# Sliding-window attention into a cosine-gated feed-forward: the opening rewritten as one list of steps, with the first two token tiles in halves

## The chip, the cores and the metric

The kernel runs on one core of a Trainium2 chip. A core has TensorE (PE, matrix multiplies into PSUM), VectorE (DVE), ScalarE (ACT, functions such as exponential and sine), GpSimd (POOL) and SyncE (SP), each with its own instruction stream in order, and 16 DMA engines that move data on request of a queue. GpSimd's queue can convert f32 to bf16 on the way; SyncE's queue copies and transposes. The metric is the device time of one execution in microseconds. The kernel before takes 308.19 us, the median of 3 runs (308.08 to 308.48).

## What is computed

Eight batches, eight heads of 64, 576 tokens each. Every token attends to itself and the 63 tokens before it; the heads of a token are then put side by side and go through two matrix products with a gate between them.

```python
scores = scale * np.matmul(q, k.transpose(0, 1, 3, 2))      # q, k, v: (8, 8, 576, 64) f32
mask = (rel >= 0) & (rel < 64)                               # rel = query position - key position
scores = np.where(mask, scores, -1000000000.0)
attn = softmax(scores)                                       # max subtracted, exp, divided by the sum
x = matmul(attn, v).transpose(0, 2, 1, 3).reshape(4608, 512)
h = x @ w_in                                                 # w_in (512, 2048)
out = (h * np.cos(h)) @ w_out                                # w_out (2048, 512)
```

## The kernel before

**Tiles.** The 4608 tokens are cut into nine tiles of 512 for the feed-forward. Attention works in units of 64 queries against 128 keys for two heads at once (a "pair", four pairs); a batch has nine units per pair, so that tile 1 covers the last 64 tokens of batch 0 and the first 448 of batch 1. Three or four units make a group, and a group passes through these steps, each a function: scores (`g_scores`, `burst`, PE), negated row maximum (`g_max`, DVE), exponential with row sums (`g_exp`, ACT), reciprocal (`g_inv`, DVE), normalisation to bf16 `w` (`g_norm`, GpSimd or DVE), transposition of `w` to `wT` (`g_trans`, on PE with a copy out of PSUM by `g_put`, or by SyncE's DMA). Then `values` multiplies by v into `o_ps` and `put_x` copies that to `xT`, the feed-forward's input.

**Feed-forward.** For each of 16 blocks of 128 columns of w_in, four matmuls of 512 tokens (`first`, L351) make h in a PSUM bank; ACT takes the sine of h + pi/2 (L507), DVE multiplies it with h (the gate, L510) into `gT`. Then 16 matmuls for each 128 tokens (L522) give the output, which is copied out of PSUM and stored. Five named PSUM banks (X0, X1, S, O0, O1) and three taken in turn ("t") are shared by all of this.

**Order.** Everything is scheduled by hand: what one engine does follows the order in which the program issues it. From tile 1 on, the steps of the next batch's attention are put into a plan with due times (`at`), and `pump` issues what is due after each sine block or four output matmuls. The opening, which has nothing to hide behind, is the string `FIRST` (L41): steps of batch 0's attention in order, such as `s.0.1` (scores of pair 0, second group), `m`, `e`, `i`, `n`, `w`, `c` (the steps above), `tq`/`tk` and `pq`/`pk` (transposition of q and k on PE, copy out of PSUM), `z` (v shifted by 64 tokens, by DVE or GpSimd), `v` and `x` (values, xT), `h` (three or more first-layer blocks over one pair), `l` (the next load), `tb` (table of the sine).

**Batch 0 before.** All q, k and v rows come by GpSimd's queue, cast on the way, pair by pair for batch 0; q is scaled when it is copied out of PSUM. The causal window is added on PE: a matmul of `ident` with `mask16` (L238) starts each group's PSUM bank, and `g_max` is a plain reduction (L273); the exponential reads the scores in PSUM. For batch 1 on, `g_max` (L277) adds the mask and takes the maximum at once, writing `s` to SBUF, from where the exponential reads. Loads of w_in come in three pieces after v, then q and k of batch 1, then w_out in two, all early in GpSimd's order.

**Tile 0 and 1 before.** Tile 0's first layer starts block by block over pairs (`skewed`), its output layer runs in two halves of the 16 blocks; batch 1's scores and softmax are in the plan at fixed times during tile 0.

Of the kernel before, what the change touches and what calls it, by code (L numbers as in the profile page):

```python
# [10 lines left out]
def _safe_warn(msg, *a, **kw):  # L11
# [22 lines left out]
T = 2 * Q  # L34
LAGS = (0.2, 1, 3, 3.2, 3.8)
SKEW = 3
DIRECT = (0, 1, 2, 3, 8, 9)
# [14 lines left out]
def kernel(  # L52
# [35 lines left out]
    mask16 = const.tile([128, 6, 128], BF16, name="mask16")  # L88
# [7 lines left out]
    H_FIRST = ("O1", "X0", "X1", "S", "O0") * 3 + ("X0",)  # L96
    H_SECOND = ("X0", "X1", "S", "O0", "O1") * 3 + ("t",)
    H_BANKS = ("X0", "O0", "X1", "S", "O1") * 2 + ("X0", "X1", "S", "O0", "O1", "t")
    S_BANKS = ("X1", "S", "X0")
    BURSTS = (("X0", "X1", "S", "t"), ("X0", "X1", "S", "t", "t", "t"))  # L100
    S_FIRST = ("O1", "S", "O0", "X0", "X1")
# [16 lines left out]
    def put_masks():  # L118
        nc.vector.tensor_tensor(out=mask[:, 2], in0=mask[:, 0], in1=mask[:, 0], op=ALU.mult)
        nc.vector.tensor_scalar(mask[:, 1], mask[:, 2], 64.0 ** 2, NEG, ALU.is_gt, ALU.mult)  # L120
        nc.vector.tensor_scalar(mask[:, 2], mask[:, 1], -1.0, NEG, ALU.mult, ALU.add)
        nc.vector.tensor_copy(mask[:, 0, 0:64], mask[:, 2, 0:64])
        nc.vector.memset(mask[:, 0, 64:128], NEG)
        for lo, hi, of in ((0, 3, 0), (3, 5, 1), (5, 6, 1)):
            nc.scalar.copy(mask16[:, lo:hi], mask[:, of:of + hi - lo])

# [53 lines left out]
    def transposed(name, b, ps_):  # L180
# [7 lines left out]
        for p, t in zip(ps_, t_ps):  # L188
            st["t" + name, b, p] = t

    def put(name, b, p, engine=None):
        of = st.pop(("t" + name, b, p)).rearrange("d (c p) -> d p c", c=RC)
        to = halves(turned(b))[name][:, p].rearrange("d (p c) -> d p c", c=RC)
        if b or name == "k":
            copy(engine, to, of)
        elif engine == "a":
            nc.scalar.mul(to, of, scale)
        else:
            nc.vector.tensor_scalar(to, of, scale, None, ALU.mult)
# [31 lines left out]
    direct = set(range(n_first)) | {n_first + i for i in DIRECT}  # L231

    def g_scores(n, which):
        s_ps = bank(S_FIRST[which], "s_ps")
        units = groups[n]
        s_ps = s_ps[:, 0:len(units) * 128].rearrange("p (u c) -> p u c", c=128)
        m0 = 2 if units[0][2] else 0
        nc.tensor.matmul(out=s_ps.rearrange("p u c -> p (u c)"), lhsT=ident,  # L238
                         rhs=mask16[:, m0:m0 + len(units)].rearrange("p u c -> p (u c)"),
                         start=True, stop=False, skip_group_check=True)  # L240
        for u, (b, p, j) in enumerate(units):
            for h in range(2):
                d = slice(64 * h, 64 * h + 64)
                nc.tensor.matmul(out=s_ps[d, u].rearrange("p (a t) -> p a t", a=2), lhsT=q_cols(b, p, j)[d],
                                 rhs=k_cols(b, p, j)[d], start=False, stop=u == len(units) - 1, skip_group_check=True)
        st["s", n] = s_ps
        st.update({("cross", unit): 0 for unit in units})


    def burst(n0, banks):  # L250
        for i in range(0, len(banks), 2):
            pair = [groups[n0 + i], groups[n0 + i + 1]]
# [3 lines left out]
            for u in range(len(pair[0])):  # L256
                for cross in range(2):
# [6 lines left out]
                    st["cross", (b, p, j)] = cross ^ (p % 2 if b == 1 else 0)  # L264
            for cross in range(2):
                st["s", n0 + i + cross] = s_ps[cross]


    def g_max(n):
        s_ps, units = st["s", n], groups[n]  # L270
        negm = att.tile([128, GF], F32, tag="negm", name="negm", bufs=8)
        if n < n_first:
            nc.vector.tensor_reduce(out=negm[:, 0:len(units)], in_=s_ps, op=ALU.max, axis=AX.X, negate=True)  # L273
        else:
            s = att.tile([128, GF, 128], F32, tag="s", name="s", bufs=4)
            for u, (b, p, j) in enumerate(units):
                nc.vector.tensor_tensor_reduce(out=s[:, u], in0=s_ps[:, u], in1=mask[:, 2 - j % 2 if j else 0],  # L277
                                               scale=-scale if b else -1.0, scalar=BIG, op0=ALU.add, op1=ALU.min,
                                               accum_out=negm[:, u:u + 1])
            st["s", n] = s  # L280
        st["m", n] = negm

    def g_exp(n):
        s, negm = st.pop(("s", n)), st.pop(("m", n))
        e = att.tile([128, GF, 128], F32, tag="e", name="e", bufs=6)
        den = att.tile([128, GF], F32, tag="den", name="den", bufs=8)
        for u in range(len(groups[n])):
            nc.scalar.activation(e[:, u], s[:, u], AF.Exp, bias=negm[:, u:u + 1], scale=1.0 if n < n_first else -1.0,  # L288
# [3 lines left out]
    def g_inv(n):  # L292
        e, den = st["e", n]
        rden = att.tile([128, GF], F32, tag="rden", name="rden", bufs=8)
# [40 lines left out]
    def put_x(mt, p, engine=None):  # L335
        if ("xT", mt) not in st:
            st["xT", mt] = att.tile([128, PAIRS, MT], BF16, tag="xT", name="xT", bufs=2)
        o_ps = st.pop(("o", mt, p))
        copy(engine, st["xT", mt][:, p], o_ps)
# [8 lines left out]
    def first(mt, ff, ks, start, stop):  # L348
        if start:
            st["h", ff] = bank((H_FIRST, H_SECOND, H_BANKS)[min(mt, 2)][ff], "h_ps")  # L350
# [3 lines left out]
    def skew(mt):  # L354
        return 5 if mt == 1 else SKEW

    def skewed(mt, ks, n):
        for ff in range(skew(mt)):
# [206 lines left out]
```

## Time and profile before

| | |
|---|---|
| median of 3 runs | 308.19 us (308.08 to 308.48) |
| the profiled execution | 308.04 us, span 306.0 us |
| PE busy | 294.1 us, 96% |
| ACT busy | 235.6 us, 77% |
| DVE busy | 219.3 us, 72% |
| GpSimd busy | 171.9 us, 56% |
| moved by DMA | 43.58 MB, mean 142 GB/s |

In a timeline row the first number is the start from the span's begin, the second how long the instruction or the merged run of instructions took, then engine, line, operation, output<-input, shapes, count, and in brackets the idle time before it and what released it. In a row of the chain the second number is the time that this piece holds the chain. In a row of DMA issues the last number is the time from issue to landing. Matmuls are pipelined, so their listed durations overlap; their spacing tells what one costs. A row of a stretch of time lists the busy time of PE, weight loads, DVE, ACT and GpSimd with their counts, the granted TensorE clock as a share of full speed, the DMA share and the GB/s.

### The profile page before, as it was taken

How to read it: one execution, taken by the hardware profiler on the slowest of the kernel's cores; microseconds unless marked ns; L12 is line 12 of the kernel's file. 1: busy time of each engine (PE TensorE's matmuls, PEld its weight loads, DVE VectorE, ACT ScalarE, POOL GpSimd, SP SyncE). 2: the span in 40 equal slices, each digit the busy share in tenths (PEclk: the TensorE clock that was granted, in tenths of full speed). 3: DMA queues.
4: the chain of work that ended last, by engine and by line, in shares of the span. 5: the costliest groups of instructions: out<-in, count | busy, mean ns of one | idle time of the engine just before them, and what ended most of it. 6: DMA issues, size and time to landing. Idle time of an engine off the chain costs nothing.

```text
span 306.0 us, 7884 instructions
## 1 busy us (share of the span) xinstructions
PE 294.1 (96%) x2668; PEld 143.1 (47%) x2668; DVE 219.3 (72%) x832; ACT 235.6 (77%) x786; POOL 171.9 (56%) x200
## 2 busy tenths in 40 slices
PE   3979999999999999999999999999999999999996
PEld 2645444444444444444454445444544454454443
DVE  2796889678787778777878787788778877235701
ACT  4798689977997799879986998699869987106600
POOL 8997237889465976497759765957533630000000
PEclk9989999999999999999999999999999999999999
DMA  6999999599969999999999999999993441011012
GB/s 83 167 211 207 208 168 161 79 179 166 238 110 159 180 197 135 164 149 219 145 170 161 213 141 170 161 216 120 171 170 117 88 130 61 0 72 70 0 69 71
DMA packets 165577, 43.58 MB, mean 142 GB/s; under 512 B 154720, under 2 KB 161056, under 8 KB 165536
## 3 DMA queue, kind: packets, MB, share of 16 engines
q0 software_dynamic: 99632, 18.36, 75.4%
q1 hardware_dynamic: 65760, 24.52, 39.9%
q8 instruction: 21, 0.34, 0.5%
q10 hardware_dynamic: 144, 0.20, 0.2%
q14 instruction: 20, 0.16, 0.2%
HBM read 36.70 MB, written 9.44 MB: 151 GB/s over the span
## 4 chain that ended last, share of the span: by engine, by line
PE 83%; ACT 5%; DVE 5%; DMA 3%; POOL 1%; issue 1%; POOLq 0%; DVEq 0%
PE h_ps L351 41%; PE out_ps L522 33%; ACT e L288 3%; PE o_ps L330 3%; PE s_ps L261 3%; DMA rows<-in_q_dram 1%; PE out_ps L366 1%; DVE s L277 1%; DMA wT<-w 1%; DVE negm L273 1%; DVE w L302 1%; ACT L343 1%; PE tk_ps L186 1%; PE tq_ps L186 1%; POOL w L302 1%
## 5 line engine op out<-in xcount | busy, mean ns | idle before, releaser
L351 PE MATMUL h_ps<-xT,w_in 128*128 128x512 bf16 x576 | 128.1, 381 | 0.9 <-ACT xT L109 0.5
L522 PE MATMUL out_ps<-w_out,gT 128*128 128x512 bf16 x560 | 125.1, 379 | 0.2 <-DVE gT L510 0.2
L510 DVE TENSOR_TENSOR gT<-h_ps,sin 128x512 bf16<-128x512 f32 x144 | 95.5, 689 | 35.4 <-ACT sin L507 35.2
L507 ACT ACTIVATE sin<-h_ps 128x512 f32<-128x512 f32 x144 | 83.0, 599 | 34.2 <-PE h_ps L351 33.0
L288 ACT ACTIVATE e<-s,negm 128x128 f32<-128x128 f32 x256 | 98.6, 387 | 0.3 <-DVE negm L277 0.3
L302 POOL TENSOR_TENSOR w<-e,rden 128x512 bf16<-128x512 f32 (+1 forms) x76 | 74.3, 992 | 32.4 <-DVE rden L295 30.3
L351 PEld LDWEIGHTS <-w_in 128*128 128x128 bf16 x576 | 55.9, 98 | 66.7 <-issue 2.0
L522 PEld LDWEIGHTS <-gT 128*128 128x128 bf16 x560 | 53.2, 98 | 62.4 <-issue 0.2
L277 DVE CUSTOM_DVE_ANT_0 s<-s_ps,mask 128x128 f32<-128x128 f32 x256 | 58.1, 285 | 0.4 <-PE s_ps L261 0.4
L288 ACT ACTIVATION_READ_ACCUMULATOR e<-s,negm 128x1 f32 x256 | 48.0, 188 | 0.0
L149 POOL DMA_DIRECT2D rows<-in_q_dram x30 | 25.4, 866 | 25.3 <-DMA T<-rows 15.5
L162 POOL DMA_DIRECT2D v<-in_v_dram x35 | 29.6, 869 | 12.4 <-DMA rows<-in_k_dram 5.8
L109 ACT COPY out_sb<-out_ps 128x512 f32<-128x512 f32 (+1 forms) x18 | 10.1, 561 | 24.4 <-PE out_ps L522 19.0
L295 DVE RECIPROCAL rden<-den 128x4 f32<-128x4 f32 (+1 forms) x80 | 13.8, 172 | 18.3 <-ACT e L288 17.1
L149 POOL DMA_DIRECT2D rows<-in_k_dram x30 | 25.5, 898 | 0.5 <-DMA T<-rows 0.5
L109 DVE CAST xT<-o_ps 128x512 bf16<-128x512 f32 x26 | 16.9, 681 | 6.5 <-PE o_ps L330 6.2
L277 DVE DVE_READ_ACCUMULATOR2_ANT negm<- 128x1 f32 x256 | 21.3, 83 | 0.0
L109 DVE COPY out_sb<-out_ps 128x512 f32<-128x512 f32 x18 | 12.4, 689 | 12.0 <-PE out_ps L522 12.0
L288 ACT ACTIVATE e<-s_ps,negm 128x128 f32<-128x128 f32 x32 | 11.4, 394 | 1.6 <-DVE negm L273 1.4
L261 PE MATMUL s_ps<-T 64*64 64x128 bf16 x512 | 12.1, 221 | 0.0
L261 PEld LDWEIGHTS <-T 64*64 64x64 bf16 x512 | 8.2, 106 | 8.3 <-DVE negm L277 3.9
L330 PEld LDWEIGHTS <-v 128*64 128x64 bf16 x504 | 9.7, 114 | 4.4 <-issue 2.3
(54 smaller groups left out, 148.9 us busy)
## 6 DMA issues: line engine op xcount, KB each, us to landing
out_dram<-out_sb SPq DMA_DIRECT2D x16, 512.0 KB, 6.9
v<-in_v_dram POOLq DMA_DIRECT2D x28, 128.0 KB, 8.3
rows<-in_q_dram POOLq DMA_DIRECT2D x24, 128.0 KB, 5.9
rows<-in_k_dram POOLq DMA_DIRECT2D x24, 128.0 KB, 9.0
w_out<-in_moe_w_out_dram POOLq DMA_DIRECT2D x2, 1024.0 KB, 16.8
w_in<-in_moe_w_in_dram POOLq DMA_DIRECT2D x2, 768.0 KB, 12.1
wT<-w SPq DMA_TRANSPOSE x66, 3.8
out_dram<-out_sb SPq DMA_DIRECT2D x3, 256.0 KB, 2.0
```

Of the source, the lines that this page charges most:

```text
L109: {"a": nc.scalar.copy, "p": nc.gpsimd.tensor_copy}.get(engine, nc.vector.tensor_copy)(out, in_)
L149: nc.gpsimd.dma_start(out=rows(b)[lo:lo + n, slot * 512:slot * 512 + 512].rearrange("p (h d) -> p h d", h=H), in_={"q": q, "k": k}[name][b ...
L162: nc.gpsimd.dma_start(out=vt.rearrange("p (h d) -> p h d", h=H), in_=v[b, :, c * 128:c * 128 + n, :].rearrange("h p d -> p h d"))
L261: nc.tensor.matmul(out=s_ps[cross][to, u].rearrange("p (a t) -> p a t", a=2), lhsT=q_cols(b, p, j)[d], rhs=k_cols(b, p, j)[d], start=True, ...
L277: nc.vector.tensor_tensor_reduce(out=s[:, u], in0=s_ps[:, u], in1=mask[:, 2 - j % 2 if j else 0], scale=-scale if b else -1.0, scalar=BIG, ...
L288: nc.scalar.activation(e[:, u], s[:, u], AF.Exp, bias=negm[:, u:u + 1], scale=1.0 if n < n_first else -1.0, accum_out=den[:, u:u + 1])
L302: (nc.gpsimd if engine == "p" else nc.vector).tensor_tensor(out=w[:, 0:u], in0=e[:, 0:u], op=ALU.mult, in1=rden[:, 0:u].unsqueeze(2).to_br ...
L330: nc.tensor.matmul(out=o_ps[64 * h:64 * h + 64, 64 * i:64 * i + 64], lhsT=values_of(b)[:, max(j - 1, 0), 128 * p + 64 * h:128 * p + 64 * h ...
L351: nc.tensor.matmul(out=st["h", ff], lhsT=w_in_sb[:, ks, ff * 128:ff * 128 + 128], rhs=st["xT", mt][:, ks], start=start, stop=stop)
L507: nc.scalar.activation(sin, h_ps, AF.Sin, bias=math.pi / 2.0)
L510: nc.vector.tensor_tensor(out=gt[:, e], in0=h_ps, in1=sin, op=ALU.mult)
L522: nc.tensor.matmul(out=o_ps[e], lhsT=gT[ff // 2][:, ff % 2, ms * 128:ms * 128 + 128], rhs=w_out_sb[:, ff], start=ff == 0, stop=ff == n_ff - 1)
```

## The change

The opening becomes one list that reaches through tile 0, batch 1's attention and the first blocks of tile 1; a function `step` reads each token of it, loads included.

- Tiles 0 and 1 go through values, xT, first layer, sine and gate in halves of 256 tokens, with two blocks of 128 columns in one bank (`half_values`, `half_x`, `half_first`, `half_sin`, `half_gate`). Tile 0 takes its second half first. A half block is 8 matmuls of 256 columns; sine and gate still handle 512 columns at once. Its token `hh` issues the two pairs that come first, `hi` the other two. Tile 0's output layer is issued by fours of blocks (`o.ms.part`), between batch 1's scores.
- k and q of pair 0 are loaded as f32 by SyncE (`k0h`, `q0h`) into an output tile and cast to bf16 by ACT (`ck0:a`, `cq0:a`).
- The mask matmul and `mask16` go; batch 0 uses the masked maximum and reads `s` in SBUF like the others, and q is not scaled on its way any more.
- v of batch 0 is shifted by SyncE's DMA in three parts (`z.1`, `z.0`, `z.2`).
- w_in and w_out are loaded in quarters (`wi0` to `wi3`, `wo0` to `wo3`). `wi0` and `wi1` follow v's chunks 2, 3, 1; `wi3`, then batch 1's k and q (`kB`, `qB`), then `wi2` stand between normalisations on GpSimd; then come chunks of batch 2's q and k, w_out and batch 1's v (`vB`).
- Six of batch 1's groups for tile 1 have `w` transposed by DMA (`BY_DMA`), four groups for tile 1 on PE; before it were six on PE.

```diff
-DIRECT = (0, 1, 2, 3, 8, 9)
+BY_DMA = (11, 12, 13, 15, 16, 17)
 FIRST = (
...
+    "k0h q0h k1 id q1 q3 iota ck0:a k3 cq0:a tk.0 q2 pk.0:d tq.0 k2 tk.1 pq.0:a v2 mask pk.1:a s.0.1:O1 v3 tq.1 "
+    "m.0.1 s.0.0:X0 pq.1:a v1 tq.3 m.0.0 e.0.1 s.1.1:X1 wi0 tk.3 m.1.1 s.1.0:S wi1 pq.3:a pk.3:d tq.2 e.1.1 i.0.1 "
+    "s.3.1:O0 pq.2:d n.0.1:p tk.2 m.3.1 pk.2:a v0 w.0.1 s.2.1:O1 i.1.1 e.3.1 c.0.1:d n.1.1:p s.2.0:X0 m.2.1 z.1 "
+    "w.1.1 i.3.1 e.2.1 m.2.0 n.3.1:p s.3.0:X1 c.1.1:d w.3.1 e.0.0 i.2.1 m.3.0 n.2.1:p v.0.1 wi3 c.3.1:a w.2.1 "
+    "x.0.1:d e.2.0 c.2.1:d hh.0.1:O0 i.0.0 hh.1.1:O1 m.1.0 n.0.0:p v.1.1 e.3.0 hh.2.1:X0 x.1.1:d kB w.0.0 i.2.0 "
+    "z.0 hh.3.1:X1 n.2.0:d e.1.0 qB hi.0.1 hi.1.1 c.0.0:d wi2 w.2.0 i.3.0 hi.3.1 i.1.0 tb n.3.0:p n.1.0:d hi.2.1 "
+    "hh.7.1:S c.2.0:d q2c4 w.1.0 sin.0.1 w.3.0 c.1.0:d k2c4 hi.7.1 sin.2.1 g.0.1 v.0.0 sin.1.1 c.3.0:d q2c3 "
+    "hh.6.1:O0 v.1.0 x.0.0:a g.1.1 wo0 hi.6.1 sin.7.1 g.2.1 hh.0.0:O1 v4 sin.6.1 Bk.0 x.1.0:d hh.1.0:X0 wo1 "
...
+    "x1.0.1:a w1.18 v1.1.1 sn1.4 x1.1.1:a g1.4 w1.19 sn1.3 g1.3 g1.2 "
 )
...
     def g_scores(n, which):
-        nc.tensor.matmul(out=s_ps.rearrange("p u c -> p (u c)"), lhsT=ident,
-                         rhs=mask16[:, m0:m0 + len(units)].rearrange("p u c -> p (u c)"),
-                         start=True, stop=False, skip_group_check=True)
...
     def g_max(n):
-        if n < n_first:
-            nc.vector.tensor_reduce(out=negm[:, 0:len(units)], in_=s_ps, op=ALU.max, axis=AX.X, negate=True)
...
+            nc.vector.tensor_tensor_reduce(out=s[:, u], in0=s_ps[:, u], in1=mask[:, 2 - j % 2 if j else 0],
+                                           scale=-scale, scalar=BIG, op0=ALU.add, op1=ALU.min,
+                                           accum_out=negm[:, u:u + 1])
...
+    def half_values(mt, pp, a):
+        st["o", mt, pp, a] = o_ps = ps_t.tile([128, 2, MT // 2], F32, tag="t", name="o_ps")
...
+    def half_x(mt, pp, a, engine):
+        copy(engine, x_tile(mt)[:, 2 * pp:2 * pp + 2, 256 * a:256 * a + 256], st.pop(("o", mt, pp, a)))
+
+    def half_first(mt, i, a, which=None, parts=(0, 1)):
+        if 0 in parts:
+            st["h", mt, i, a] = bank(which, "h_ps").rearrange("p (s t) -> p s t", s=2)
+        for s_ in range(2):
+            for ks in [2 * part + o for part in parts for o in range(2)]:
+                ff = 2 * i + s_
+                nc.tensor.matmul(out=st["h", mt, i, a][:, s_], lhsT=w_in_sb[:, ks, ff * 128:ff * 128 + 128],
+                                 rhs=st["xT", mt][:, ks, 256 * a:256 * a + 256], start=s_ == ks == 0, stop=ks == PAIRS - 1,
+                                 skip_group_check=True)
+
+    def half_sin(mt, i, a):
+        st["sin", mt, i, a] = sin = moe.tile([128, 2, MT // 2], F32, tag="sin", name="sin", bufs=4)
+        nc.scalar.activation(sin, st["h", mt, i, a], AF.Sin, bias=math.pi / 2.0)
...
+    def first_out(ms, part, which=None):
+        for ff in range(4 * part, 4 * part + 4):
+            nc.tensor.matmul(out=st["out", ms], lhsT=st["gT", 0, ff // 2][:, ff % 2, ms * 128:ms * 128 + 128],
+                             rhs=w_out_sb[:, ff], start=ff == 0, stop=ff == n_ff - 1)
...
+    def first_spread(part):
+        vt = vtiles[0]
+        for lo, hi, a, b in ((0, 64, *((1, 2), (3, 7), (7, 7))[part]), (64, 128, *((1, 2), (3, 7), (7, 8))[part])):
+            if a < b:
+                nc.sync.dma_start(out=vt[lo:hi, a:b:2], in_=vt[lo:hi, a + 1 - lo // 32:b + 1 - lo // 32:2])
+
+    def load_f32(name):
+        st[name, "f32"] = moe.tile([128, 2, d_model], F32, tag="out", name="first_f32", bufs=3).rearrange("p a b -> p (a b)")[:, 0:S]
+        nc.sync.dma_start(out=st[name, "f32"], in_={"q": q, "k": k}[name][0, 0:2].rearrange("h (p c) d -> (h p) (c d)", c=RC))
+
+    def cast(name, engine):
+        copy(engine, halves(rows(0))[name][:, 0], st.pop((name, "f32")))
...
+    for token in FIRST.split():
+        step(token)
...
+        if mt == 1:
+            last = ('O1', 'X1', 'S', 'X0', 'O0') + ("S", "X0", "O0", "X1", "O1", "X0", "S", "X1", "O0", "O1", "t")
+            for nth in range(n_ff):
+                a, i = divmod(nth, n_ff // 2)
+                if nth > 4:
+                    half_first(1, i, a, last[nth])
+                    half_sin(1, i, a)
+                    if nth == n_ff - 1:
+                        exp_table()
+                    half_gate(1, i, a)
+                pump(base + nth)
```

310 lines of the change are left out of this document (158 added, 152 removed), and 17 rows, old and new, of the table FIRST.

## The prediction

> **What bounds the kernel now.** I read the chain that ended last first, then TensorE's (PE's) timeline of the opening, then ScalarE's, VectorE's and the load queue's. The chain, in order of time (start, us, what):
>
> ```profile
> 26.21 5.77 PE h_ps L351 x26
> 31.98 0.41 PE tq_ps L186 x36
> ...
> 57.70 0.17 PE tw_ps L311 x3
> ...
> 58.73 0.63 PE o_ps L330 x32
> ...
> 92.21 13.92 PE h_ps L351 x64
> 106.13 0.57 PE s_ps L261 x32
> ...
> 111.99 0.92 PE s_ps L261 x38
> ...
> 123.02 13.97 PE h_ps L351 x64
> ```
>
> From tile 2 on the chain is PE without a gap: a tile takes 123.02 - 92.21 = 30.8 us, 64 first-layer matmuls take 13.97, so 0.218 each. Nothing after tile 1's first layer is edited, so whatever the edit does shows as a shift of that layer's end. PE's timeline gives that end and where the opening loses (bracket: idle before it, and its releaser):
>
> ```profile
> 26.21 5.77 PE L351 MATMUL h_ps<-xT,w_in 128*128 128x512 bf16 x26 [0.51 <-ACT xT L109]
> ...
> 74.97 0.64 PE L261 MATMUL s_ps<-T 64*64 64x128 bf16 x32
> ```
>
> Tile 1's first layer ends at 74.97. Between 26.21 and there PE has 122 first-layer and 64 output matmuls (186 x 0.218 = 40.5), four sets of 36 transposes (4 x 0.41 = 1.6), batch 1's scores (84 at (0.57 + 0.92)/72, 1.7), two sets of o_ps (2 x 0.63 = 1.3) and 20 w transposes (20 x 0.17/3 = 1.1): 46.2 in 48.8 us. Only 2.6 us are lost there; the rest of the loss lies before 26.21, where PE waits for batch 0's attention. What paces that is ScalarE (ACT):
>
> ```profile
> 8.30 0.37 ACT L288 ACTIVATE e<-s_ps,negm 128x128 f32<-128x128 f32 x1 [1.45 <-DVE negm L273]
> ...
> 15.69 0.65 ACT L109 COPY T<-tk_ps 128x576 bf16<-128x576 bf16 x1
> ...
> 21.83 0.36 ACT L288 ACTIVATE e<-s_ps,negm 128x128 f32<-128x128 f32 x1
> ...
> 22.17 0.37 ACT L288 ACTIVATE e<-s_ps,negm 128x128 f32<-128x128 f32 x1
> ...
> 22.51 0.60 ACT L109 COPY wT<-tw_ps 128x512 bf16<-128x512 bf16 x1
> ...
> 24.19 1.28 ACT L346 ACT_TABLE_LOAD   x1
> ...
> 27.27 2.75 ACT L507 ACTIVATE sin<-h_ps 128x512 f32<-128x512 f32 x5 [0.62 <-PE h_ps L351]
> ...
> 43.41 0.39 ACT L288 ACTIVATE e<-s,negm 128x128 f32<-128x128 f32 x1
> ```
>
> Its 32 exponentials begin at 8.30 and its first sine runs at 27.27; 19 us for 11 us of exponentials (0.34 apart).
>
> The sum is made on the profiled execution: 308.04 us, span 306.0 and 2.0 around it; the median of the runs is 308.19, so 0.15 is no matter.
>
> **The change, part by part.**
>
> *First pair by SyncE as f32.* PE starts on q's first rows at 4.82 now. After the edit SyncE issues k, then q, as its first work, by my estimate 0.75 and 1.4 into the span, and ACT casts each (0.65, as its T copy above). The rows next to it:
>
> ```profile
> 4.82 0.69 PE L186 MATMUL tq_ps<-ident,rows 64*64 64x64 bf16 x18 [4.82 <-DMA rows<-in_q_dram]
> ...
> rows<-in_q_dram POOLq DMA_DIRECT2D x4, 144.0 KB, 5.0
> ...
> out_dram<-out_sb SPq DMA_DIRECT2D x3, 256.0 KB, 2.0
> ...
> v<-v SPq DMA_DIRECT2D x1, 256.0 KB, 6.2
> ...
> 12.60 0.75 DVE L109 COPY T<-tk_ps 128x576 bf16<-128x576 bf16 x1
> ```
>
> Landing is bounded by 2.0 and 5.0; I take 2.3, nearest SyncE's own quiet transfer. k is there at 3.1, cast 3.9, transposed 4.6 (0.69), put by VectorE 5.4 (0.75); q follows 0.7 behind, the first scores end near 6.9.
>
> *Masks.* Eight mask matmuls go from PE, but PE is waiting there, so I cost that at nothing. The reductions become masked ones:
>
> ```profile
> 7.58 0.69 DVE L273 TENSOR_REDUCE negm<-s_ps 128x4 f32<-128x512 f32 x1 [1.27 <-PE s_ps L244]
> ...
> 42.63 0.28 DVE L277 CUSTOM_DVE_ANT_0 s<-s_ps,mask 128x128 f32<-128x128 f32 x1
> ...
> 42.84 0.29 DVE L277 CUSTOM_DVE_ANT_0 s<-s_ps,mask 128x128 f32<-128x128 f32 x1
> ...
> 77.09 0.39 ACT L288 ACTIVATE e<-s,negm 128x128 f32<-128x128 f32 x1
> ...
> 77.48 0.39 ACT L288 ACTIVATE e<-s,negm 128x128 f32<-128x128 f32 x1
> ```
>
> Four at 0.21 are 0.85 against about 0.6 (the 0.69 overlaps its neighbour): +2 us over eight groups on VectorE, which loses the 1.48 v copy (below); up to the last group's reciprocal it has eight maxima (6.8), two T copies, three wT copies, two xT casts, a normalisation and the reciprocals, some 13 us from 6.9 on, done by 20, so ACT stays last. The exponentials now read s in SBUF, 0.385 apart instead of 0.34: 32 x 0.04 = +1.3 us on ACT, on the path. First group's max ends 7.75, ACT is on a T copy until 8.2: first exponential 8.2, as before. With the loads' bounds, 7.9 to 10.9.
>
> *ACT to its first sine.* 32 x 0.385 = 12.3; T copies of pair 3's q and pair 2's k, 1.3; one wT copy 0.6; table and dummy 1.4; about 1 us of waiting for pair 2 and 3's transposes. 8.2 + 16.6 = 24.8. The mask casts, two wT copies and the xT casts that stood there go to VectorE or behind the sines. Gain at this point 2.5 us, if PE has h in PSUM by then.
>
> *v by DMA.* VectorE's 1.48 copy and GpSimd's other half of it go; SyncE moves the slots instead, and v's second half-product waits for it (z.1):
>
> ```profile
> 18.52 1.48 DVE L109 COPY v<-v 64x1536 bf16<-64x1536 bf16 x1
> ...
> 45.83 1.36 SPq L170 DMA_DIRECT2D v<-v  x2
> ```
>
> v chunks 1 to 3 are issued by about 8.0; six 144 KB loads and these three of 128 KB, at the 0.7 of each (2.9 per 576 KB, below) from about 4.8 on, land near 11.5; two shifts, 0.68 to issue each, land 2.0 to 6.2 after: 15 to 19.5. I take 17.5, nearer 6.2, whose queue was also shared. Behind it on PE stand a w transpose set and all first-layer work, on VectorE x.0.1, then the max of the last group (m.1.0). That must be done when ACT wants it at 21.7; back through 0.85, a wT copy 0.36, a reciprocal 0.1, x.0.1 0.68 and o_ps 0.5, z.1 may land at 19.2. So it is hidden, with 1.7 us to spare; past that each microsecond costs one. The Trainium skill bears on this: "DMA: Bandwidth & Descriptors", § Queues, rings and completion order, says that each DMA engine alternates packet by packet between the queues that have work. By it the shift would not stand behind the weights' whole backlog but share with it, about the 6.2 above; no run here yet shows it in the opening.
>
> *Halves.* Twice as many first-layer matmuls of 256 columns in tiles 0 and 1, twice the weight loads. The nearest rows are the last ones, 16 of 384 and 16 of 128 columns:
>
> ```profile
> L351 PEld LDWEIGHTS <-w_in 128*128 128x128 bf16 x576 | 55.9, 98 | 66.7 <-issue 2.0
> ...
> 299.45 3.51 PE out_ps L366 x32
> ```
>
> 3.51/32 = 0.110 for 256 columns on average, against 0.109 for half of 512: 256 x 0.001 = 0.3 us in all. A weight load of 98 ns just fits under it. From below it is nothing; from above 256 x 0.1 = 26 us if loads did not overlap at all, which the 128-column rows exclude.
>
> *PE from 24.8.* By then 4.5 of tile 0's 16 half blocks (8 matmuls) can be in the five banks. Left: 11.5 x 0.88 = 10.1; o_ps 0.6; two w sets 0.5; batch 1's transposes 1.6; its scores 1.7; 14 w transposes 0.8; 64 output matmuls 14.0; tile 1's o_ps 1.3; its first layer 14.1. Together 44.7, end at 69.5 without a stall; with the 2.6 us that the same stretch loses now, 72.1. ACT keeps up: 16 sines at 0.55 (2.75/5), four T copies at 0.65, an xT 0.6 and a table 1.4 are 13.4, so its 40 exponentials start near 38.2 against 43.41; 15.4 more, 53.6; an xT copy and table, 55.7. PE reaches tile 1's halves at about 57.
>
> *Moved past GpSimd's queue.* The third w_in quarter, batch 1's k and q and the last w_in quarter are issued behind normalisations (1.08 each), no longer at 12.66 to 14.95:
>
> ```profile
> 12.66 0.81 POOL L175 DMA_DIRECT2D w_in<-in_moe_w_in_dram  x1
> 13.46 0.76 POOL L142 DMA_DIRECT2D rows<-in_q_dram  x1
> 14.19 0.77 POOL L142 DMA_DIRECT2D rows<-in_k_dram  x1
> 14.95 1.08 POOL L302 TENSOR_TENSOR w<-e,rden 128x512 bf16<-128x512 f32 x1
> ...
> rows<-in_q_dram POOLq DMA_DIRECT2D x1, 576.0 KB, 15.0
> rows<-in_k_dram POOLq DMA_DIRECT2D x1, 576.0 KB, 17.1
> ```
>
> q and k of batch 1 land at 13.46 + 15.0 = 28.5 and 14.19 + 17.1 = 31.3: 2.8 to 2.9 us per 576 KB, 2.6 per 512. In the new order the third quarter waits for pair 2's normalisation (16.5, when ACT has done four groups, to 17.7). What was issued before has landed by 17.9; with the same start-up as the first load (about 2.5 us without its own bytes) the queue runs dry for 2.4 us, then lands the quarter at 22.9, k 25.8, q 28.7, the last quarter 31.4. PE asks for k after its seventh half block (28), for q at 31, for the quarter (hh.4.1) at 32.5. So it costs nothing, with 1 to 2 us of cover; without cover each microsecond late is one on PE. Behind come three small chunks (1.4), four w_out quarters (10.4), a v chunk and three of q (2.5), to 45.7, and v of batch 1 to 48.6; its shift, 0.65 + 6.2, to 55.4, for a use near 56: the thinnest cover.
>
> Sum: 72.1 - 74.97 = -2.9; 308.04 - 2.9 = 305.1, told as 305.0, since the uncertainty of the 2.6 is far more than the tenth.
>
> **The rivals.**
>
> *No stall at all.* PE ends tile 1's first layer at 69.5 to 70: 308.04 - 5.2 = 302.8. For it: each arrival worked out above comes before its use. Against: the present list loses 2.6 with all its loads long landed.
>
> *Half clock.* After PE's idle stretch the clock granted was halved:
>
> ```profile
> 18.00:20.00 2.00, 0.52 (x9) 0.37 (x8) 2.00 (x4) 2.00 (x11) 1.92 (x3) 1.00 1.17 212
> 20.30:23.60 3.30, 3.05 (x38) 1.88 (x31) 2.89 (x8) 2.71 (x15) 3.28 (x5) 0.50 1.15 208
> ```
>
> (PE busy 0.52 of 2 us, then clock 0.50 for at least 3.3 us.) The wait for z.1 leaves PE as idle, later; if the half-clock stretch falls after 24.8, where PE works without slack, it costs 3.4/2 = 1.7 us: 305.0 + 1.7 = 306.7. The Trainium skill, "TensorE: Matmul & The Clock Gate", § HAM oscillation, has the rule that speaks against this edit: idle gaps above about 3.4 us put the clock back to half. The trace agrees in kind, though its gap at 18 to 20 is shorter.
>
> *v's second shift.* It sets tile 1's start: landing at 60 instead of 55, 60 + 14.6 = 74.6 and nothing is gained: 307.9. It takes the loads to slip by 5 us; each microsecond short of that still leaves one of gain.
>
> *The loads behind the normalisations* (slower). If issue to landing stays at the 15.0 of now instead of shrinking with the backlog, k lands at 20.6 + 15 = 35.6, PE and ACT stand still for 7.6 us at Bk.0, and 308.04 + 7.6 - 3.0 gives 312.6. It decides from 5 us of lateness on (28 + 3). For it: 15.0 and 17.1 are measured; against: those waited for older transfers, and 144 KB at an emptier queue took 5.0.
>
> **How the numbers follow.** A measurement tells 0.2% (0.6 us) from no change. Chances: forecast 0.46 (its own range 303.6 to 306.2), no stall 0.14, half clock 0.14, v's shift 0.08, late loads 0.18. Faster: 0.46 + 0.14 + 0.14 = 0.74; same: half of the v case and a little, 0.05; slower: the late loads and the rest, 0.21. The range reaches to the no-stall time and through the milder part of the late loads: 302.2 to 309.2, leaving out under 0.2.
>
> **What would show it.** First exponential at 8 to 8.5; first sine at 24 to 26; no PE wait on rows of batch 1 or w_in; half blocks 0.88 us; batch 1's exponentials from about 38; tile 1's first layer ended at 71 to 73 and then the old spacing of 30.8. Wrong it is if PE waits for v, rows or w_in by more than 2 us, or if a first sine near 25 still ends in 75: then something between 38 and 57 takes the gain back.

## The result, and the profile after

The changed kernel takes 320.13 us, the median of four runs (318.48 to 320.76), against 308.34 for the kernel before beside it (308.08 to 308.75): a ratio of 1.0373, 95% interval 1.033 to 1.0416. It is slower by 11.8 us; 305.0 was forecast and 309.2 was the end of the range. The profiled execution took 319.69 us with a span of 317.8, which is 11.65 more than the 308.04 of before.

From the page of the changed kernel, busy times, granted clock and chain by engine:

```profile
PE 289.4 (91%) x2751; PEld 154.9 (49%) x2782; DVE 219.8 (69%) x886; ACT 237.4 (75%) x786; POOL 169.8 (53%) x199
...
PEclk9958999959999999999999999999999999999999
...
PE 80%; DMA 8%; DVE 4%; ACT 3%; issue 2%; POOL 2%; SPq 0%; POOLq 0%
```

PE is busy 4.7 us less than before, so no work was added to it. The clock has two dents instead of one, in the third and the ninth slice, and 8% of the chain is now transfers, 3% before. Its longest pieces in the opening (start, us, what):

```profile
6.60 5.86 DMA v<-in_v_dram
13.29 6.78 DMA v<-v
...
57.83 8.73 DMA v<-v
...
77.68 8.91 PE h_ps L355 x80
...
166.11 10.74 PE h_ps L394 x49
...
196.96 10.74 PE h_ps L394 x49
```

Two copies of v by SyncE are on the chain for 15.5 us. Behind them the spacing of a tile is 196.96 - 166.11 = 30.85, as before. PE's timeline shows what the copies do to it:

```profile
20.20 0.64 PE L336 MATMUL o_ps<-wT,v 128*64 128x64 bf16 x16 [4.52 <-DMA v<-v]
...
66.70 0.90 PE L336 MATMUL o_ps<-wT,v 128*64 128x64 bf16 x26 [7.47 <-DMA v<-v]
...
77.68 8.91 PE L355 MATMUL h_ps<-xT,w_in 128*128 128x256 bf16 x80 [1.64 <-DVE gT L366]
86.52 0.64 PE L257 MATMUL s_ps<-T 64*64 64x128 bf16 x32
```

PE waits 4.52 us for the shifted v of batch 0 and 7.47 for that of batch 1. Tile 1's first layer ends at 77.68 + 8.91 = 86.59 instead of 74.97, which is 11.62: the whole loss is made by then. Two stretches of time (PE, weight loads, DVE, ACT, GpSimd busy; then the clock, the DMA share, GB/s) show the clock around each wait:

```profile
16.00:26.00 10.00, 5.55 (x57) 4.08 (x58) 4.25 (x23) 7.67 (x33) 4.80 (x6) 0.51 1.02 156
60.00:69.00 9.00, 1.97 (x29) 1.38 (x31) 2.24 (x5) 1.44 (x4) 0.93 (x1) 0.69 1.49 162
```

The queues say why the copies are late. SyncE's issues before, then after, GpSimd's after, and the time to landing of SyncE's copies after, from the timelines and from the list of transfers:

```profile
52.95 5.19 SPq L314 DMA_TRANSPOSE wT<-w  x4
58.50 8.47 SPq L153 DMA_TRANSPOSE T<-rows  x2
```

```profile
12.54 9.69 SPq L469 DMA_DIRECT2D v<-v  x5
47.64 6.67 SPq L159 DMA_TRANSPOSE T<-rows  x1
54.42 2.53 SPq L307 DMA_TRANSPOSE wT<-w  x2
57.12 1.33 SPq L176 DMA_DIRECT2D v<-v  x2
```

```profile
22.08 1.03 POOL L295 TENSOR_TENSOR w<-e,rden 128x512 bf16<-128x512 f32 x1 [4.56 <-DVE rden L288]
23.07 0.80 POOL L148 DMA_DIRECT2D rows<-in_k_dram  x1
...
45.08 0.87 POOL L168 DMA_DIRECT2D v<-in_v_dram  x1 [1.67 <-DMA w_out<-in_moe_w_out_dram]
```

```profile
first_f<-in_k_dram SPq DMA_DIRECT2D x1, 288.0 KB, 2.8
first_f<-in_q_dram SPq DMA_DIRECT2D x1, 288.0 KB, 3.1
v<-v SPq DMA_DIRECT2D x2, 128.0 KB, 6.6
v<-v SPq DMA_DIRECT2D x1, 256.0 KB, 8.7
...
v<-v SPq DMA_DIRECT2D x1, 192.0 KB, 7.8
```

The first shift's two halves are issued as the chunks of v that each reads land (12.46 and 13.2) and need 6.4 and 6.8 us. Batch 1's shift was issued at 45.83 before, ahead of every w transpose and of the turning of the following batch's rows (`T<-rows`). Now the last chunk that it reads is asked for at 45.08 and lands 9.1 us later, at 54.2. SyncE turns q's rows (token `turnq`) from 47.64 on, 6.67 us, then issues two w transposes, and only then, at 57.12, the shift; its larger half lands at 57.83 + 8.73 = 66.56. (The fifth chunk of v, asked for at 52.63, does not hold the shift: the copies neither read nor write its rows, and they are issued before it lands, 8.3 us later at 60.9.)

### The profile page after: what moved, and what is told of

It is laid out like the page before. It is cut to its first block, busy times and chain, and to the rows that moved or that the text cites. A ratio compares the mean times of both kernels' runs of the same rounds, so it can differ in the third digit from the quotient of the medians.

```text
span 317.8 us, 8113 instructions
## 1 busy us (share of the span) xinstructions
PE 289.4 (91%) x2751; PEld 154.9 (49%) x2782; DVE 219.8 (69%) x886; ACT 237.4 (75%) x786; POOL 169.8 (53%) x199
## 4 chain that ended last, share of the span: by engine, by line
PE 80%; DMA 8%; DVE 4%; ACT 3%; issue 2%; POOL 2%; SPq 0%; POOLq 0%
PE out_ps L594 31%; PE h_ps L394 31%; PE h_ps L355 9%; DMA v<-v 5%; PE s_ps L257 3%; PE o_ps L323 2%; ACT e L281 2%; DMA v<-in_v_dram 2%; DVE s L270 1%; DMA wT<-w 1%; PE out_ps L406 1%; POOL rows L148 1%; PE o_ps L336 1%; DVE w L295 1%; DVE out_sb L118 1%
## 5 line engine op out<-in xcount | busy, mean ns | idle before, releaser
L281 ACT ACTIVATE e<-s,negm 128x128 f32<-128x128 f32 x288 | 111.0, 388 | 1.7 <-DVE negm L270 1.7
L594 PE MATMUL out_ps<-w_out,gT 128*128 128x512 bf16 x482 | 107.7, 379 | 1.5 <-issue 1.1
L394 PE MATMUL h_ps<-xT,w_in 128*128 128x512 bf16 x435 | 97.5, 379 | 0.8
L594 PEld LDWEIGHTS <-gT 128*128 128x128 bf16 x496 | 47.4, 98 | 56.7
L394 PEld LDWEIGHTS <-w_in 128*128 128x128 bf16 x448 | 43.6, 98 | 52.1 <-issue 0.6
L270 DVE CUSTOM_DVE_ANT_0 s<-s_ps,mask 128x128 f32<-128x128 f32 x288 | 65.1, 285 | 1.0 <-PE s_ps L257 0.7
L281 ACT ACTIVATION_READ_ACCUMULATOR e<-s,negm 128x1 f32 x288 | 54.4, 189 | 0.0
L168 POOL DMA_DIRECT2D v<-in_v_dram x35 | 29.9, 865 | 11.8 <-DVE negm L270 4.1
L355 PE MATMUL h_ps<-xT,w_in 128*128 128x256 bf16 x256 | 32.7, 284 | 2.0 <-DVE gT L366 1.6
L355 PEld LDWEIGHTS <-w_in 128*128 128x128 bf16 x256 | 25.1, 102 | 6.7 <-DVE gT L366 1.9
L118 ACT COPY out_sb<-out_ps 128x512 f32<-128x512 f32 (+1 forms) x16 | 9.0, 562 | 24.2 <-PE out_ps L594 18.7
L288 DVE RECIPROCAL rden<-den 128x4 f32<-128x4 f32 (+1 forms) x80 | 13.4, 171 | 17.7 <-ACT e L281 17.3
L270 DVE DVE_READ_ACCUMULATOR2_ANT negm<- 128x1 f32 x288 | 24.1, 84 | 0.0
L118 DVE COPY out_sb<-out_ps 128x512 f32<-128x512 f32 x20 | 13.7, 687 | 12.6 <-PE out_ps L594 12.0
```

Of the source, the lines that this page charges most:

```text
L118: {"a": nc.scalar.copy, "p": nc.gpsimd.tensor_copy}.get(engine, nc.vector.tensor_copy)(out, in_)
L168: nc.gpsimd.dma_start(out=vt.rearrange("p (h d) -> p h d", h=H), in_=v[b, :, c * 128:c * 128 + n, :].rearrange("h p d -> p h d"))
L355: nc.tensor.matmul(out=st["h", mt, i, a][:, s_], lhsT=w_in_sb[:, ks, ff * 128:ff * 128 + 128], rhs=st["xT", mt][:, ks, 256 * a:256 * a + 2 ...
L394: nc.tensor.matmul(out=st["h", ff], lhsT=w_in_sb[:, ks, ff * 128:ff * 128 + 128], rhs=st["xT", mt][:, ks], start=start, stop=stop)
L594: nc.tensor.matmul(out=o_ps[e], lhsT=gT[ff // 2][:, ff % 2, ms * 128:ms * 128 + 128], rhs=w_out_sb[:, ff], start=ff == 0, stop=ff == n_ff - 1)
```

## The experiments

In the list of steps an edit is shown by its tokens; where a shift is moved off SyncE, the helper also takes the engines (`p` GpSimd, `d` VectorE) of the two halves:

```diff
-                nc.sync.dma_start(out=vt[lo:hi, a:b:2], in_=vt[lo:hi, a + 1 - lo // 32:b + 1 - lo // 32:2])
+                to, of = vt[lo:hi, a:b:2], vt[lo:hi, a + 1 - lo // 32:b + 1 - lo // 32:2]
+                if engines[lo // 64] == "s":
+                    nc.sync.dma_start(out=to, in_=of)
+                else:
+                    copy(engines[lo // 64], to, of)
```

Single times (a1 to c4, d4, e1, f1, f2, f5) are of the profiled execution and stand beside a kernel before at 307.9 to 308.3. Ten executions of d1 lie up to 3.2 us apart, so a difference of 2 us between two single times is only as good as the waits in the timelines that go with it.

**The first shift alone** (a1):

```diff
-z.1 z.0 z.2
+z.1:pd z.0:dd z.2:dd
```

> The changed kernel with one edit: batch 0's v is shifted by GpSimd and VectorE copies instead of SyncE's DMA. Theory 1 (the late shifts are the cause): the PE wait of 4.5 us at 15.7 to 20.2 goes, the half-clock stretch that follows it shortens, the first sine comes at 24.5 to 25 instead of 26.6, GpSimd's normalisation at 22.1 and the loads behind it come 3 us earlier; the second shift is still behind the DMA transposes of SyncE, so 314 to 317 us. Theory 2 (the list, the 256-column halves and the exponentials from SBUF are slow themselves): within 1 us of 320.

**The second shift alone** (a2):

```diff
-zB
+zB:pd
```

> The changed kernel with one edit: batch 1's v is shifted by GpSimd (odd slots' lower half) and VectorE (upper half) at the same place in the list. Theory 1: the PE wait of 7.5 us before 66.7 goes together with the half clock after it, tile 1's first layer ends 8 to 10 us earlier: 309.5 to 312. Theory 2: PE finds the next wait in the same place, 316 or more.

**Both** (a3), the two edits together:

> Both edits at once, so no v of batches 0 and 1 is shifted by DMA. Theory 1: the two gains add up and the forecast's sum holds: 304 to 307. Theory 2: 309 or more, slower than the kernel before although no shift waits.

**The shift by DMA in the kernel before** (b1), `z.1.p` and `z.0.d` there made `z.1.dma` and `z.0.dma`:

> The kernel before with one part of the change alone: batch 0's v shifted by SyncE's DMA, two DMAs issued when v's four chunks have landed (15.4). Theory 1: they land 6 to 7 us later, 22, so tile 0's first o_ps (19.8 now) waits 2 to 3 us and PE's half clock lasts longer: 310.5 to 313. Theory 2: hidden, within 0.6 of 308.

The times are 317.64, 317.99, 313.46 and 313.34. PE's timeline in a1, a2, a3 and b1, one fence each:

```profile
64.19 0.90 PE L336 MATMUL o_ps<-wT,v 128*64 128x64 bf16 x26 [7.86 <-DMA v<-v]
```

```profile
20.05 0.64 PE L336 MATMUL o_ps<-wT,v 128*64 128x64 bf16 x16 [4.12 <-DMA v<-v]
...
62.25 0.44 PE L336 MATMUL o_ps<-wT,v 128*64 128x64 bf16 x16 [1.38 <-DMA wT<-w]
65.03 0.37 PE L336 MATMUL o_ps<-wT,v 128*64 128x64 bf16 x6 [2.33 <-DMA wT<-w]
```

```profile
61.38 0.37 PE L336 MATMUL o_ps<-wT,v 128*64 128x64 bf16 x6 [1.57 <-DMA wT<-w]
```

```profile
25.89 0.96 PE L330 MATMUL o_ps<-wT,v 128*64 128x64 bf16 x28 [7.59 <-DMA v<-v]
```

Each of these shifts by DMA costs time: 2.1 and 1.7 us in the changed kernel, and 5.4 in the kernel before (against the 307.9 beside it), where PE's wait is 7.59 and not the 2 to 3 that were expected. a1 and b1 came a little above the ranges of their first theory, a2 and a3 as their second theory said: neither shift is the whole. With the first gone the second wait is as long as ever (7.86), and with both gone a wait on SyncE's w transposes stands in the same place. SyncE's timeline in a3 has these six behind the turned rows:

```profile
44.99 6.71 SPq L159 DMA_TRANSPOSE T<-rows  x1
51.76 12.13 SPq L307 DMA_TRANSPOSE wT<-w  x6
```

The opening itself came as forecast or earlier once the first shift was off SyncE: a3's first sine was at 23.82, its first output matmul at 39.09, 2.8 us ahead of before.

**SyncE's order.** c1 is a3 with the turn of q moved back beside that of k, behind the w transposes; c2 is a3 with two of the six w groups transposed on PE; c3 does both; c4 is a1 with the turn moved back, the second shift by SyncE.

```diff
-e1.13 turnq
+e1.13
...
-h1.0:X1 turnk
+h1.0:X1 turnq turnk
```

```diff
-BY_DMA = (11, 12, 13, 15, 16, 17)
+BY_DMA = (12, 13, 16, 17)
...
-w1.11
+w1.11 c1.11:d
...
-w1.15
+w1.15 c1.15:d
```

> The run with both shifts on VectorE and GpSimd (313.46) with one more edit: SyncE's first transposition of batch 2's rows (T<-rows, 6.7 us to issue) is issued beside the second one, behind the six wT transposes of tile 1 instead of ahead of them. Theory 3 (SyncE's queue of transposes sets tile 1's start): PE's waits on wT<-w (0.7 and 1.6 us) and the half clock behind them go, first layer of tile 1 starts 2 to 4 us earlier, 309 to 311.5. Theory 4 (the exponentials and normalisations on ACT, DVE and GpSimd set it): within 1 us of 313.5.

> The run with both shifts on engines, and the two groups (11, 15) of tile 1's first half that went by DMA transpose are transposed on PE and copied by VectorE. Theory 3: no wT transpose stands before tile 1's first half, 308.5 to 311. Theory 4: within 1 us of 313.5.

> Both of these edits together. Theory 3: no better than the better of the two by more than 0.7 us, since both take the same wait away; 308 to 310.5. Theory 4: within 1 us of 313.5.

> As the first of these runs, but batch 1's v is shifted by SyncE's DMA as in the changed kernel (batch 0's still by engines). If the second shift was late because it stood behind T<-rows in SyncE's queue, it is issued when v has landed (52) and lands at 58 to 59, so 310 to 312; if the DMA itself is what is slow, it lands after 61 and the time is 313 or more.

Measured: 309.5, 309.83, 310.29 and 310.43. All four are within their ranges. Either way of relieving SyncE takes the same wait away, some 3.5 to 4 us, and they do not add up: it is the w transposes behind the turned rows. Two things make these late, and c1 to c3 do not separate them. They are issued later, and they land more slowly while the rows are on their way: a3's six need 7.6 us in the median from issue to landing, c1's 3.9. c4 against a1 (317.64) is one edit, and worth 7.2 us: the shift is issued at 52.11 instead of 54.95, and its larger half lands 5.2 us after its issue instead of 8.4.

**The rest of the distance to before.** In c1 PE still waits 1.64 us for a gate. d1 moves that gate's token (`g1.2`) forward; d4 is d1 with the first pair by GpSimd's queue again; d5 is d1 with the slots that `z.1` shifts loaded a second time from memory instead of copied, and chunk 1 of v later; e1 is the changed kernel with the loads `wi0` and `wi1` behind the first shift.

```diff
-g1.0 x1.0.1:a w1.18 v1.1.1 sn1.4 x1.1.1:a g1.4 w1.19 sn1.3 g1.3 g1.2
+g1.0 g1.2 x1.0.1:a w1.18 v1.1.1 sn1.4 x1.1.1:a g1.4 w1.19 sn1.3 g1.3
```

> As the kernel with both shifts on engines and batch 1's q turned late (309.5), with the gate of tile 1's bank X0 moved forward in the list. If the 1.64 us that PE waits for that gate's copy inside tile 1's first layer is only its place in the list, PE's first layer of tile 1 has no wait above 0.5 us, ends near 74.3 instead of 75.97, and the time is 307.9 (307.4 to 308.5). If the gate waits for its sine instead, the wait stays and the time is 309.3 to 309.7.

> The d1 kernel with the first pair's q and k loaded by GpSimd's casting queue again, without the two casts on ScalarE: prices that part of the change alone. The f32 pair landed at 2.8 and 3.1 but cost two 0.65 casts; the first exponential stood at 8.1 after and at 8.3 before. Expected: first exponential 0.1 to 1.0 later, first sine 0 to 0.8 later, total from 0.3 less to 1.0 us more than d1. If the part is what brings the opening forward, the loss is over 1.5.

> The d1 kernel with batch 0's odd slots of v loaded straight from memory by GpSimd's queue, in place of the copy by GpSimd and VectorE that followed the load. That takes some 1.5 us from VectorE and a shared stretch from GpSimd before the last softmax group, and moves 128 KB ahead of w_in. If VectorE's work there paces the opening, the first sine comes 0.5 to 1.0 earlier and the time is 306.5 to 307.6; if ScalarE's exponentials pace it alone, the time is within 0.4 of d1; if the four smaller loads delay w_in, PE waits for it near 24 and the time is up to 1.5 worse.

> The changed kernel with its first two loads of w_in issued only after the second half-product of pair 1, so that nothing of GpSimd's load queue is in flight beside the first shift of v. If the shift's landing (6.4 and 6.8 us) is the price of sharing the DMA engines with those loads, each 128 KB half lands within 2.5 to 4 us of its issue and PE starts the second half-product at 16 to 17.5 instead of 20.2. If the landing is the price of such a copy by itself, it stays at 6 to 7 and the start stays near 20. The whole time is no better either way, 318 to 323, since w_in arrives some 3 us later and the second shift is untouched.

d1 took 310.41 us (ratio to before 1.0089, 1.0058 to 1.012): its expectation missed. From its timeline of PE:

```profile
64.45 9.78 PE L355 MATMUL h_ps<-xT,w_in 128*128 128x256 bf16 x88
76.03 0.64 PE L257 MATMUL s_ps<-T 64*64 64x128 bf16 x32 [1.79 <-DMA T<-rows]
```

The gate's wait is gone and the layer ends at 64.45 + 9.78 = 74.23, ahead of before; then PE waits for the rows, which SyncE turns last. The stall had only covered the next one. d4 took 312.85 in its one run: its layer ends at 78.90 - 1.76 = 77.14 against 74.23, and its first exponential comes 1.0 later (9.24), so the f32 pair is worth up to 2.9 us, more than was expected (d1's ten runs lie between 309.49 and 312.72, so one time says less than the layer's end). d5 took 310.51 (1.007, 1.0042 to 1.0099): its four smaller loads made PE wait 1.48 us for w_in, as its third case said, but its median is only 0.1 above d1's, which fits the second case as well.

e1 took 319.78 as a whole, and tells what the first shift's 6.6 us are. From its transfers, then PE's timeline:

```profile
v<-v SPq DMA_DIRECT2D x2, 128.0 KB, 3.8
```

```profile
17.00 0.64 PE L336 MATMUL o_ps<-wT,v 128*64 128x64 bf16 x16 [1.08 <-DMA v<-v]
...
22.55 1.89 PE L355 MATMUL h_ps<-xT,w_in 128*128 128x256 bf16 x8 [4.37 <-DMA w_in<-in_moe_w_in_dram]
```

Without the two queued loads of 512 KB the same copies land in 3.8 us and PE starts at 17.00 instead of 20.20; what is gained there is lost to w_in. The shift and the weights want the DMA engines in the same microseconds, and neither of the two orders tried makes both early.

**The parts put together.** f1 is the changed kernel with only the turn of q moved back. f2 is c4 with the gate early, and with batch 1's chunks of v loaded where the list loads the following batch's q and k chunks (and these where v was), so that `zB` can go early. f3 is f2 with c2's two groups on PE.

```diff
-q2c4 k2c4 q2c3 q2c2 q2c1
+vB0 vB1 vB2 vB3 vB4
...
-vB1 vB2 vB0 vB3 vB4
+q2c4 q2c3 q2c2 q2c1 k2c4
...
-o.0.0:S
+o.0.0:S zB
...
-m1.17 zB
+m1.17
```

> The changed kernel with one edit: the turning of batch 1's next q rows is issued on SyncE beside that of k, behind the second shift of v and the six w transposes, instead of ahead of them. If SyncE's order is a cause by itself, the wait of 7.5 us on v in batch 1 shrinks to 1 to 3.5 and the time falls by 6 to 8, to 311.5 to 313.7. If the wait is made by the late loads of v alone, it stays above 5 and the time is above 317.

> First shift by engines, q's turn late, the gate of bank X0 early, and the five chunks of batch 1's v loaded where the list loads tile 2's q and k chunks (and these where v was), with the second shift issued by SyncE as soon as the list allows. If the second shift's lateness or its 2.0 us on VectorE was the rest, PE has no wait above 0.6 us on v or w before tile 1's first layer, that layer ends near 72.5 to 73.5, and then PE waits up to 2 us for the turned rows behind six w transposes: 307.0 to 309.0. If it was not, the time stays at 309.5 to 310.5.

> The kernel with v's chunks first, and two of the six weight groups of batch 1 transposed on PE instead of by SyncE, so that SyncE turns the rows some 4 us earlier. If SyncE's six transposes hold the rows back, no wait for the turned rows is left at tile 1's end; PE pays 8 small transposes (0.5 us) and VectorE two copies: first layer of tile 1 ends near 73 to 74 and the time is 306.0 to 307.5, better than the kernel before. If the rows were not held back by them, the time is that of the kernel with v's chunks first or up to 0.7 worse.

f1 took 313.82, 0.1 above its range: the single moved token is worth 5.9 us in the changed kernel. PE's timeline, then SyncE's, in f1:

```profile
62.48 0.60 PE L336 MATMUL o_ps<-wT,v 128*64 128x64 bf16 x26 [2.68 <-DMA v<-v]
```

```profile
51.33 5.08 SPq L307 DMA_TRANSPOSE wT<-w  x2
56.59 1.33 SPq L176 DMA_DIRECT2D v<-v  x2
57.97 5.86 SPq L307 DMA_TRANSPOSE wT<-w  x4
64.06 9.57 SPq L159 DMA_TRANSPOSE T<-rows  x2
```

The shift is issued hardly earlier than in the changed kernel (56.59 against 57.12). With the rows gone from its front, it stands behind the second w transpose, whose w VectorE has ready at 55.20; the last chunk that the shift reads had landed at 53.5. But its larger half lands within 5.0 us instead of 8.7, and the fifth chunk of v, on GpSimd's queue, within 2.9 instead of 8.3: in the changed kernel the turned rows, 13.3 us from issue to landing, were on their way beside them. So of the 4.2 us by which the shift lands earlier (62.34 against 66.56), 0.5 come from SyncE's order of issue and 3.7 from quicker landing. What is left of the wait, 2.68, is less than the 3.1 us that the shift stands in SyncE's queue after its v has landed. f2 loads these chunks earlier and puts the shift ahead of the w transposes, at 44.51; it has no wait for v and reaches 308.48. Which of its two moves was needed no run tells. From its timeline of PE:

```profile
72.86 0.64 PE L257 MATMUL s_ps<-T 64*64 64x128 bf16 x32
...
91.19 1.01 PE L323 MATMUL o_ps<-wT,v 128*64 128x64 bf16 x52 [2.25 <-DMA wT<-w]
```

In f2 tile 1's first layer ends 2.1 us ahead of before, and nothing of it reaches the end: tile 2 then waits 2.25 us for w transposes that SyncE issues from 80.37 on, as late as before (80.15). f3 took 308.3 (1.0009, 0.9989 to 1.003), level with before and above the expected 306 to 307.5. Its ten runs lie between 307.21 and 309.27; the profiled one is the fastest, and in it PE still waits 0.73 us for the rows and 0.34 for w transposes. What the slower runs wait for is not shown.

**A version a little ahead.** f4 is f3 with q turned in a gap of SyncE's queue, behind `w1.13`, and two more groups on PE; f5 only turns q there.

```diff
-BY_DMA = (12, 13, 16, 17)
+BY_DMA = (12, 13)
...
-e1.18 w1.13
+e1.18 w1.13 turnq
...
-o.2.3 x1.1.0:a
+o.2.3 x1.1.0:a c1.17:a
...
-h1.0:X1 turnq turnk
+h1.0:X1 turnk c1.16:a
```

> Values first, with four of the six weight groups of batch 1 transposed on PE and the turn of q issued between SyncE's two transposes and that of k, in the 4.7 us in which SyncE is idle now. If SyncE's queue is what holds back the rest, PE waits for neither the turned rows nor tile 2's w transposes, tile 1's first layer ends near 73.3 to 74 (8 more transposes, 0.4 us) and the time is 305.5 to 307.0, faster than the kernel before. If tile 2's transposes wait for their softmax instead of for SyncE, the wait at the start of tile 2 stays at 1 to 2.3 us and the time is 307.5 to 308.5.

> Values first, two groups on PE as in the run before, with only the turn of q moved ahead of the last two of SyncE's four transposes. If the turn's 6.7 us of issue on SyncE delays what stands behind it, PE waits 1 to 3 us for those two groups at 61 to 64, as it waited for the second shift in the changed kernel, and the time is 308 to 310. If the transposes do not need that queue then, it is 306 to 307.5.

f4 took 307.4 us against 308.01: 0.9981, interval 0.9968 to 0.9993. That is 0.6 us ahead of the kernel before, with an interval that just leaves out no change, and 0.4 above the expected range. f5 took 307.9 in one run, just under its first case, with one wait of 0.86 us on a w transpose behind the turn where 1 to 3 were expected. PE's timeline, then SyncE's, in f4:

```profile
56.42 0.69 PE L336 MATMUL o_ps<-wT,v 128*64 128x64 bf16 x32
...
64.15 9.78 PE L355 MATMUL h_ps<-xT,w_in 128*128 128x256 bf16 x88
73.86 0.64 PE L257 MATMUL s_ps<-T 64*64 64x128 bf16 x32
...
89.27 1.49 PE L323 MATMUL o_ps<-wT,v 128*64 128x64 bf16 x64
```

```profile
55.48 5.71 SPq L159 DMA_TRANSPOSE T<-rows  x2
```

PE waits neither for v nor for the turned rows nor for SyncE's w transposes any more; tile 1's first layer ends at 73.86, 1.1 us before the 74.97 of the kernel before, and the profiled run, the fastest of its ten, is that much shorter (306.9 against 308.04). The medians lie 0.6 apart.

## Why the prediction was wrong

In the order of its steps.

*First pair by SyncE: right.* The pair landed 2.8 and 3.1 us after issue, within 2.0 to 5.0, and the first exponential came at 8.11 against 8.2. The price of the part without it, as d4 shows, had not been asked.

*Masks: right.* The exponentials stand 0.385 apart, and in the kernels without the first wait ACT reaches its first sine at 23.8 to 24.2 (a1, a3, f2, f4), 0.6 to 1.0 us ahead of the 24.8 forecast. In the changed kernel it is 26.59:

```profile
22.27 0.40 ACT L281 ACTIVATE e<-s,negm 128x128 f32<-128x128 f32 x1 [1.74 <-DVE negm L270]
...
26.59 0.60 ACT L361 ACTIVATE sin<-h_ps 128x512 f32<-128x512 f32 x1 [1.16 <-PE h_ps L355]
...
44.61 0.39 ACT L281 ACTIVATE e<-s,negm 128x128 f32<-128x128 f32 x1
```

*v by DMA: the term z.1 was mis-sized.* It took 17.5 from bounds of 15 to 19.5 (its own terms add up to 14.9 to 19.1), with 19.2 as the last harmless moment; measured are 18.9 and 20.07. Two links were off: the chunks that it reads landed at 12.5 and 13.2 and not 11.5, and both halves took more than the upper price of 6.2 (6.4 and 6.8 us). The cause lay in the bounds: the quiet end, 2.0, had no claim on a copy beside a megabyte of queued weights, which e1 shows by itself (3.8 without them). The Trainium skill's rule in "DMA: Bandwidth & Descriptors", § Queues, rings and completion order, that a DMA engine alternates by packets between queues, was cited for sharing; e1's 3.8 against 6.6 agrees with sharing. The prediction then chose a middle value although sharing was what it expected.

*And its price per microsecond was too low.* A missed 0.9 was to cost 0.9. The clock drops to half without this wait too, but in a1 it is full again between 20 and 21, in the changed kernel between 25 and 26 (0.51 from 16 to 26, the rival of half clock). The wait also held GpSimd's normalisation at 22.08, behind which batch 1's k, q and the last quarter of w_in are issued. ACT's first sine is 1.8 late by it. Taking the first shift off SyncE is worth 2.1 us in the changed kernel (a1) and 3.4 once the second wait is shorter (c4 against f1).

*Halves: right.* 80 matmuls in 8.84 us (77.68 to 86.52) are 0.1105 each.

*ACT "keeps up", exponentials from 38.2: wrong.* This step added up ACT's own work, 13.4 us from the first sine. But the last sine waits for the last half block, so PE paces it: from the prediction's own terms PE needs 10.1 + 0.6 + 0.5 + 1.6 and part of the scores from 24.8 on, which is past 38, and a sine and the table of 1.4 come behind. f4, where no wait of PE is put down to a transfer, starts these exponentials at 41.32. Since tile 1's values still come when forecast (56.42 against "about 57"), the later start used up slack, not time. Of the 72.1 forecast for the end of tile 1's first layer, f2's 72.86 is the nearest that was seen.

*The "thinnest cover", batch 1's shift: the step that failed.* The sum gave v landed at 48.6, "its shift, 0.65 + 6.2, to 55.4, for a use near 56", as if SyncE's queue were empty and nothing else moved. Measured are v landed at 54.2, the shift issued at 57.12 and landed at 66.56, and each part has its share of the 11.1 us. The loads of v are 5.6 late; 2.6 of that is the first wait handed on, as a1, without it, has them at 51.6. SyncE's order, which was not read, adds 2.9: the turned rows and two w transposes stand ahead of the shift, where before it stood ahead of them. The landing, 9.4 from the first issue instead of 6.85, adds 2.6, with a transfer of 13.3 us beside it. Of the turned rows f1 shows that, with the first wait in place, they cost more by this than by the order: 3.7 against 0.5; without it (c4 against a1) the two are 3.2 and 2.8. The rival "v's second shift" had the place right, gave it 5 us to slip and 0.08: it slipped 11. (Its own figures give 307.7 for a landing at 60, not 307.9.)

*Loads behind the normalisations: hardly.* k of batch 1 landed at 28.8 and q at 31.7, 3 us after the forecast, with PE as late; neither makes PE wait. The step looked for PE waiting on these rows; what the slip made late was the tail of the same queue, v.

*"Whatever the edit does shows as a shift of that layer's end": wrong for a gain.* The loss of 11.62 at the end of tile 1's first layer is the loss of the whole, but f2's gain of 2.1 there ends in tile 2's wait of 2.25. The sum carried the 2.9 to the end without asking what tile 2 waits for.

*The sum.* Following the edits from the profiled 319.69, by single times: the turn of q moved back, -5.9 (f1); the first shift off SyncE, -3.4 (c4); v's chunks and the second shift early and the gate forward, -1.9 (f2, 308.48). That is 11.2 of the 11.65. The terms depend on the order in which they are taken, as a1's 2.1 against 3.4 shows. The forecast gain of 2.9 is there in the opening (first output matmul 2.8 earlier in a3), 2.1 of it at the end of tile 1's first layer in f2, and 1.1 reaches the end in f4. Where the rest goes in f4 was not taken apart; its extra w transposes on PE are part of it.

## What to carry to other kernels

When work is given to a DMA queue, write down that queue's whole order before and after, as is done for an engine: what stands ahead of the new transfer, what that waits for, how long each takes to issue, when the source lands, and what is on its way beside it. A copy inside the chip that is quick on quiet engines is priced beside the loads that run with it, at the upper end of the rows. And a removed stall is worth little until the next queue in line is early as well: here a gate, the turned rows and the w transposes came up one after another.

## What the runs showed of the hardware

A transposing transfer holds SyncE's queue while it is issued: that of q's rows took 6.67 us in the changed kernel, and the w transpose behind it was issued at 54.42, against 51.33 in f1, where the rows come later. The same transfer took 4.05 us to issue in f1 and 3.78 in f4; why it varies is not shown. While it was on its way in the changed kernel, the shift of v landed 8.7 us after its issue and a 64 KB load on GpSimd's queue 8.3; in f1, without it, 5.0 and 2.9.

The clock dropped to half without one long gap. In d1 PE's longest wait since its first instruction was 1.86 us, yet (two stretches of time, the columns as above):

```profile
14.00:18.00 4.00, 2.08 (x35) 1.49 (x36) 3.63 (x21) 3.88 (x20) 3.22 (x4) 0.78 1.37 192
18.00:22.00 4.00, 3.88 (x35) 2.60 (x34) 2.74 (x15) 4.00 (x23) 3.46 (x5) 0.50 0.88 119
```

PE was busy about half of 14 to 18 and of the 4 us before (1.09 and 1.05 of 2 us each), in short pieces; the clock dropped between 16 and 17, within that longest wait, and the half clock lay on the work behind it. The Trainium skill, "TensorE: Matmul & The Clock Gate", § HAM oscillation, speaks of gaps above some 3.4 us. The changed kernel's wait of 7.47 agrees: it begins at 59.23, and the clock is full until 62 and at half from 64. Its wait of 4.52 tells nothing of this, since the clock drops as it begins (0.77 from 15 to 16, 0.50 from 16 on, the wait from 15.68). d1's stretch shows that a run of shorter gaps does it too.
